# Sharing two TensorE clusters between a pair's outputs and the next pair's scores in a retention and feed-forward kernel

## The chip, the core and the metric

The kernel runs on one core of a Trainium2 chip. The metric is the device time of one execution in microseconds (us). Six runs of the kernel before the change gave a median of 300.57 us (299.53 to 300.97).

## What is computed

Eight batches with eight heads, 576 positions, head size 64: a causal retention layer without softmax, whose scores decay with a rate of their own for each head, and a feed-forward on its output with a squared ReLU between two matrix products.

```python
scores = scale * np.matmul(q, k.transpose(0, 1, 3, 2))
gamma = 1.0 - 2.0 ** (-5.0 - np.arange(H))
Dmat = np.where(rel >= 0, gamma[:, None, None] ** rel[None, :, :], 0.0)
attn = np.matmul(scores * Dmat, v)          # then laid out as x: 4608 x 512
h = x @ w_in                                # 512 x 2048
r = np.maximum(h, 0.0)
out = (r * r) @ w_out                       # 2048 x 512
```

## The kernel before

**Units and groups.** The 4608 positions are cut into 36 units of 128 positions (L123 to L128). Four full units cover positions 0 to 511 of a batch; the last 64 positions of two batches share one tail unit. The units are handled in 19 groups (L130): two of one unit, then seventeen pairs. Within a unit the retention works on two chunks of 64 positions. It is computed by chunks: inside a chunk scores, masked and multiplied by v; between chunks a running state of 64x64 for each head, which is multiplied by q. The decay is put into v (`vdec`, when v is cast) and into the output (`gam`), so that the mask is plain ones and zeros.

**The steps of a unit.** SP loads k, q and v as fp32 (`add_load`, L255). POOL casts them to fp16 (`add_unit`, L312). For units from 8 on a transposing DMA, issued by SP too, makes `kqT`, the transposed k and q (L346); for the first eight TensorE transposes them. Loads, transposes and stores stand in one queue on SP, which issues them in order; a transpose waits there for the cast of q, a store for its output.

**The two clusters of a group** (`add_ret`, from L369). All retention matmuls are small, 64x64x64, on a quarter of the TensorE array (`quad`, L305: `row` is the half of the partitions that is read, `col` the half that is written).

- The first cluster, `fa` (L379), computes the scores (`psc`, 16 small matmuls a unit) and the sums for the state (`psS`, 16 for each full unit). VectorE (DVE) then masks the scores into `rT` (L409) and forms the states `Rm` and `R` from the sums (L426 to L436).
- The second cluster, `fb` (L461), computes the outputs (`psO`): first a part from the states (up to 16 small matmuls a pair), in which row half a writes PSUM bank 1 - a; then a drain of TensorE; then the masked scores times v, in which row half c writes bank c, with the rest of the state part. DVE multiplies the outputs by `gam` into `xT` (L509).

PSUM has eight banks. Four belong to the feed-forward (`ps_ff`). The other four are two tiles of two banks of one kind, `pr` (`ps_ret`, L152), shared by scores, sums and the outputs of each unit.

**The feed-forward** (`add_ff`, L557). The first product (`ph`, L571) has 64 matmuls of 128x256 for a pair, ScalarE (ACT) applies ReLU (L579), ACT or DVE squares (L589, L591). From group 3 to group 17 the second product is done by Strassen's scheme (`add_strassen`, L630): seven products of eight matmuls of 128x256 (`po`, L664), DVE sums of their inputs (`gS`, L642), ACT and DVE putting the results together (L677, L687, L707). The other groups use the plain product (L612).

**Who sets the order.** The order on each engine is fixed when the program is built. Every piece of work is a task with an engine, a key, a planned duration, the tasks it depends on and the buffers it takes and gives back (`Schedule`, L16). `emit` plays the tasks through with the planned times: an engine that is free takes the ready task with the lowest key. The instructions are then written in the order in which the tasks started in that plan. On the chip each engine runs its own list in order, whatever the true times are. The plan counts 1.2 us for a load on SP, 2.0 for a transpose and 4.0 more until it has landed. A key counts slots: 2 x 16 slots (`L`) for a unit of the feed-forward. In `add_ret` the first cluster of a group has key `base + 3`, the second `base + 24`, with `base` two units and 20 slots (`EARLY`) ahead of the group's own feed-forward, so that the feed-forward of earlier groups stands between and around the clusters.

Of the kernel before, what the change touches and what calls it, by code (L numbers as in the profile page):

```python
# [101 lines left out]
def kernel(  # L102
# [46 lines left out]
    u_pool = ctx.enter_context(tc.tile_pool(name="u", bufs=1))  # L149
    r_pool = ctx.enter_context(tc.tile_pool(name="r", bufs=3))  # L150
    ps_ff = ctx.enter_context(tc.tile_pool(name="ps_ff", bufs=4, space=bass.MemoryType.PSUM))
    ps_ret = ctx.enter_context(tc.tile_pool(name="ps_ret", bufs=2, space=bass.MemoryType.PSUM))  # L152

    ctx.enter_context(tc.manual_schedule())

# [53 lines left out]
    WARM = 48  # L209
    EARLY = 20  # L210
    SQ_ACT = (0, 1, 2, 3, 4, 5, 6)
    XBAR = 8
    FIRST = ["u0", "u1", "u2", "u3", "w0", "w1", "w2", "w3", "w4", "w5", "w6", "w7"]
    sched = Schedule(dict(ff=4, pr=2, g=3, ld=5, wst=4, kq=7, v16=7, rT=4, x=3, rl=3, o=4, p1=1, u2=1, u4=1,
                          R=6, Rm=6, kqT=6))
    add = sched.add
    tile_of = {}
# [91 lines left out]
    def half(x):  # L309
        return slice(64 * x, 64 * x + 64)  # L310
# [55 lines left out]
            T["kqT", u].append(e)  # L366


    def add_ret(g):  # L369
        us = sorted(groups[g])  # L370
        n = len(us)
        base = (us[0] - n) * L - EARLY
        for u in us:
            add_unit(u, base - L + 4 * (u - us[0]))
        full = [u for u in us if units[u][0] == "full"]
        sc = lambda s: slice(256 * s, 256 * (s + 1))


        def fa():  # L379
            tile_of["psc", g] = ps_ret.tile([P, 2, 512], FP32, name="psc", tag="pr")  # L380
            for s, u in enumerate(us):
                kT = tile_of["kqT", u]
                ps = tile_of["psc", g][:, :, sc(s)].rearrange("p a (n i) -> p a n i", i=64)
                for hp in range(NP):
                    for a, c in ((0, 0), (1, 1), (0, 1), (1, 0)):
                        quad(ps[half(c), a, hp, :], kT[half(a), hp, half(c)], kT[half(a), NP + hp, half(c)], a, c)
            if full:
                tile_of["psS", g] = ps_ret.tile([P, 2, 512], FP32, name="psS", tag="pr")
            for s, u in enumerate(us):
                if u not in full:  # L390
                    continue
                ps = tile_of["psS", g][:, :, sc(s)].rearrange("p c (n i) -> p c n i", i=64)
                for hp in range(NP):
                    for c, a in ((0, 0), (1, 1), (0, 1), (1, 0)):
                        h = 4 * (hp // 2) + 2 * a + hp % 2
                        quad(ps[half(a), c, hp, :], tile_of["kq", u][half(c), 0, half(2 * hp + a)],
                             tile_of["v16", u][half(c), h, :], c, a)
        casts = sum((T["casts", u] for u in us), [])
        A = add("PE", base + 3, 0.2 + 0.145 * (n + len(full)), fa, deps=sum((T["kqT", u] for u in us), casts),
                acq=("pr", "pr") if full else ("pr",))  # L400
        for u in us:
            sched.free("kq", [A])


        ms = []
        for s, u in enumerate(us):
            def fm(s=s, u=u):
                t = tile_of["rT", u] = work.tile([P, 2, NP, 64], FP16, name="rT", tag="rT")
                nc.vector.tensor_tensor(  # L409
                    out=t, in0=tile_of["psc", g][:, :, sc(s)].rearrange("p a (n i) -> p a n i", i=64),  # L410
                    in1=mask.rearrange("p (o r i) -> p o r i", o=1, r=1).to_broadcast([P, 2, NP, 64]), op=ALU.mult)
            ms.append(add("DVE", base + 5 + s, 0.7, fm, deps=[A] + ms[-1:], acq=("rT",)))
        sched.free("pr", ms[-1:])


        chain = []
        for s, u in enumerate(us):
            if u not in full:
                continue
            c0 = units[u][2] == 0  # L420

            def fr0(s=s, u=u, c0=c0):
                t = tile_of["Rm", u] = st_pool.tile([P, NP * D], FP16, name="Rm", tag="Rm")
                x = tile_of["psS", g][:, 0, sc(s)]
                if c0:
                    nc.vector.tensor_copy(out=t, in_=x)  # L426
                else:
                    nc.vector.tensor_tensor(out=t, in0=x, in1=tile_of["R", u - 1], op=ALU.add)

            def fr1(s=s, u=u):  # L430
                t = tile_of["tmp", u] = work.tile([P, NP * D], FP32, name="stmp", tag="stmp", bufs=1)
                nc.vector.tensor_tensor(out=t, in0=tile_of["psS", g][:, 1, sc(s)], in1=tile_of["Rm", u], op=ALU.add)

            def fr2(s=s, u=u):
                t = tile_of["R", u] = st_pool.tile([P, NP * D], FP16, name="R", tag="R")
                nc.vector.tensor_tensor(  # L436
                    out=t.rearrange("p (n d) -> p n d", d=D), in0=tile_of["tmp", u].rearrange("p (n d) -> p n d", d=D),
                    in1=dec128.rearrange("p (n o) -> p n o", o=1).to_broadcast([P, NP, D]), op=ALU.mult)
            r0 = add("DVE", base + 5.1 + s, 0.42, fr0, deps=[A] + chain[-1:] + ([] if c0 else [T["R", u - 1]]),
                     acq=("Rm",))  # L440
            if not c0:
                T["Rread", u - 1].append(r0)
            r1 = add("DVE", base + 5.2 + s, 0.42, fr1, deps=[r0])
            r2 = add("DVE", base + 5.3 + s, 0.35, fr2, deps=[r1], acq=("R",))
            chain += [r0, r1, r2]
            T["Rm", u], T["R", u], T["Rread", u] = r0, r2, []
        if full:
            sched.free("pr", [chain[-2]])

        def states(u):
            kind, b, c = units[u]
            if kind == "tail":
                return {0: ("R", u - 5), 1: ("R", u - 1)}
            r = {1: ("Rm", u)}
            if c:
                r[0] = ("R", u - 1)
            return r

        def fb():  # L461
            begun = set()

            def put(u, c, h, lhsT, rhs, row):
                col = h % 2
                ps = tile_of["psO", u][half(col), c, half(h // 2)]
                quad(ps, lhsT, rhs, row, col, start=(u, c, col) not in begun)
                begun.add((u, c, col))

            def inter(u, other):  # L470
                st = states(u)
                for n in range(2):
                    for a, b in ((0, 0), (1, 1), (0, 1), (1, 0)):
                        c = a ^ other
                        if c in st:
                            x = 2 * n + b
                            put(u, c, 4 * n + 2 * a + b, tile_of[st[c]][half(a), half(x)],
                                tile_of["kqT", u][half(a), NP + x, half(c)], a)
            for u in us:
                tile_of["psO", u] = ps_ret.tile([P, 2, 512], FP32, name="psO", tag="pr")  # L480
                inter(u, 1)

            nc.tensor.drain()
            for u in us:
                for m in range(NP):
                    for c, b in ((0, 0), (1, 1), (0, 1), (1, 0)):
                        h = 2 * m + b
                        put(u, c, h, tile_of["v16", u][half(c), h, :], tile_of["rT", u][half(c), m % 2, 2 * (m // 2) + b, :], c)
                inter(u, 0)
        reads = [T[x] for u in us for x in states(u).values()]  # L490
        Bt = add("PE", base + 24, 0.2 + 0.29 * n, fb, deps=ms + reads, acq=("pr",) * n)
        for u in us:
            sched.free("kqT", [Bt])
            sched.free("v16", [Bt])
            sched.free("rT", [Bt])
            for name, ru in states(u).values():
                if name == "R":
                    T["Rread", ru].append(Bt)
                else:
                    sched.free("Rm", [Bt, chain[-2]])  # L500

        xs = []
        for u in us:
            s = groups[g].index(u)

            def fx(u=u, s=s):
                if ("x", g) not in tile_of:
                    tile_of["x", g] = x_pool.tile([P, NP, n * P], FP16, name="xT", tag="xT")
                nc.vector.tensor_tensor(  # L509
                    out=tile_of["x", g][:, :, s * P:(s + 1) * P].rearrange("p n (c i) -> p c n i", c=2),  # L510
                    in0=tile_of["psO", u][:, :, 0:256].rearrange("p c (n i) -> p c n i", i=64),
                    in1=gam[units[u][0]], op=ALU.mult)
            xs.append(add("DVE", base + 27 + u - us[0], 0.7, fx, deps=[Bt] + xs[-1:], acq=() if xs else ("x",)))
            sched.free("pr", xs[-1:])
            T["x", u] = xs[-1]

# [200 lines left out]
            sched.free("o", [st])  # L719

    for g in range(len(groups)):
        add_ret(g)
    for u in range(NU):
        if ("Rread", u) in T:
# [34 lines left out]
```

## Time and profile before

| what | value |
|---|---|
| median of six runs | 300.57 us (299.53 to 300.97) |
| the profiled execution, its own time | 300.97 us |
| its span, first to last instruction | 299.3 us |
| DVE, scores masked (L409), 36 times | 684 ns each |
| DVE, outputs scaled (L509), 36 times | 683 ns each |
| TensorE, small matmuls of scores, sums and outputs (L306) | 576, 512 and 1088 |
| ACT idle, waiting for `ph` | 51.0 us |
| POOL idle, waiting for v, q and k to land | 44.1, 36.4 and 31.3 us |
| transposes to `kqT`, issue to landing, median of 28 | 4.3 us |

The span is what the profile covers; 1.67 us of the execution lie around it. In the lists of groups a row has the line of the kernel, the engine, the operation and how often it ran, then busy time and the mean of one. A timeline merges neighbours of one kind: its second column runs from the first start to the last end. A TensorE matmul overlaps the next ones, so the pace is read from start to start and not from the duration of one.

### The profile page before, as it was taken

Reading aid. Unit: us, or ns where it says so; the run is one execution under the profiler, and the core shown is the slowest. Engines: PE = TensorE matmul, PEld = TensorE weight load, DVE = VectorE, ACT = ScalarE, POOL = GpSimd, SP = SyncE. Lnnn points to the kernel's source line nnn. Section 1 sums busy time; section 2 is a strip of 40 time slices with the busy share of each in tenths; the row PEclk is TensorE's granted clock in tenths of the full one; section 3 lists DMA queues with packets and bytes.
Section 4 is the critical chain, followed back from the end, with each engine's and each line's share of the span. In section 5 each row is a group of like instructions: output and inputs, shape, how many; then the busy total and the mean of one; then the engine's idle time right before and its main releaser. Section 6 shows DMA issues by size and latency. Waiting matters only on the chain.

```text
span 299.3 us, 10320 instructions
## 1 busy us (share of the span) xinstructions
PE 286.9 (96%) x4456; PEld 235.8 (79%) x4456; DVE 194.1 (65%) x409; ACT 187.0 (62%) x351; POOL 96.5 (32%) x125
## 2 busy tenths in 40 slices
PE   5986999999999999999999999999999999999995
PEld 2455964688888888888888888888888888888874
DVE  1377479785778848593959594959395959383410
ACT  4233973396667476766676666665757676657861
POOL 3433358453334151524242342334353410000000
PEclk9999999999999999999999999999999999999999
DMA  9999999889999999999999997999999960102012
GB/s 166 218 346 384 357 243 225 183 183 186 200 213 137 230 179 201 156 224 182 202 159 211 216 152 183 187 228 190 246 193 206 200 161 2 72 1 74 0 70 72
DMA packets 151742, 54.16 MB, mean 181 GB/s; under 512 B 142864, under 2 KB 143120, under 8 KB 151696
## 3 DMA queue, kind: packets, MB, share of 16 engines
q1 hardware_dynamic: 151248, 52.97, 89.8%
q8 instruction: 35, 0.57, 0.9%
q10 hardware_dynamic: 448, 0.52, 0.7%
q14 instruction: 11, 0.09, 0.1%
HBM read 36.70 MB, written 9.44 MB: 154 GB/s over the span
## 4 chain that ended last, share of the span: by engine, by line
PE 88%; DVE 7%; issue 2%; ACT 2%; POOL 0%; POOLq 0%; DVEq 0%
PE ph L571 40%; PE po L664 30%; PE psO L306 5%; PE po L612 4%; PE warm L226 4%; PE psc L306 2%; DVE wT L528 2%; PE psS L306 1%; DVE gS L642 1%; DVE gT L591 1%; ACT rl L579 1%; ACT gT L589 1%; PE psT L354 1%; DVE R L436 1%; DVE rT L409 0%
## 5 line engine op out<-in xcount | busy, mean ns | idle before, releaser
L571 PE MATMUL ph<-xT,w_in 128*128 128x256 f16 (+1 forms) x1216 | 139.5, 267 | 0.1
L571 PEld LDWEIGHTS <-w_in 128*128 128x128 f16 x1216 | 112.0, 98 | 13.6 <-POOL w_in L287 0.3
L579 ACT ACTIVATE rl<-ph 128x512 f16<-128x512 f32 x144 | 84.5, 589 | 55.6 <-PE ph L571 51.0
L589 ACT ACTIVATE gT<-rl 128x512 f16<-128x512 f16 x112 | 70.6, 630 | 3.5
L642 DVE TENSOR_TENSOR gS<-gT 128x512 f16<-128x512 f16 x60 | 31.2, 521 | 49.5 <-ACT gT L589 47.4
L332 POOL TENSOR_TENSOR v<-v,vdec_full 128x512 f16<-128x512 f32 x32 | 34.7, 1086 | 51.5 <-DMA v<-in_v_dram 40.1
L664 PEld LDWEIGHTS <-gS 128*128 128x128 f16 x480 | 46.3, 98 | 6.2 <-DVE gS L642 0.5
L664 PE MATMUL po<-wT,gS 128*128 128x256 f16 x360 | 49.1, 273 | 0.2 <-DVE gS L642 0.2
L664 PEld LDWEIGHTS <-gT 128*128 128x128 f16 x360 | 34.7, 98 | 4.2
L320 POOL CAST kq<-k 128x512 f16<-128x512 f32 x36 | 24.3, 675 | 35.8 <-DMA k<-in_k_dram 31.3
L320 POOL CAST kq<-q 128x512 f16<-128x512 f32 x32 | 22.7, 710 | 36.6 <-DMA q<-in_q_dram 36.4
L664 PE MATMUL po<-w_out,gT 128*128 128x256 f16 x240 | 31.3, 273 | 0.0
L409 DVE TENSOR_TENSOR rT<-psc,mask 128x512 f16<-128x512 f32 x36 | 24.5, 684 | 4.2 <-PE psc L306 4.2
L509 DVE TENSOR_TENSOR xT<-psO,gam_full 128x512 f16<-128x512 f32 x36 | 23.3, 683 | 3.9 <-PE psO L306 3.7
L591 DVE TENSOR_TENSOR gT<-rl 128x512 f16<-128x512 f16 x32 | 16.9, 532 | 12.9 <-ACT rl L579 12.7
L612 PE MATMUL po<-w_out,gT 128*128 128x512 f16 (+1 forms) x112 | 22.9, 349 | 0.3 <-ACT w_out L287 0.3
L677 ACT COPY u<-po 128x256 f32<-128x256 f32 x30 | 11.0, 366 | 14.6 <-PE po L664 14.5
L436 DVE TENSOR_TENSOR R<-stmp,dec 128x256 f16<-128x256 f32 x32 | 18.7, 584 | 1.0
L226 PE MATMUL warm<-junk,ident 128*128 128x512 f16 x48 | 15.0, 450 | 3.0 <-DVE junk L205 3.0
L642 DVE TENSOR_TENSOR gS<-gS,gT 128x512 f16<-128x512 f16 x30 | 16.9, 563 | 1.0
L612 PEld LDWEIGHTS <-gT 128*128 128x128 f16 x112 | 10.6, 98 | 7.7 <-issue 0.6
L687 DVE TENSOR_TENSOR o<-po,u 128x256 f32<-128x256 f32 x30 | 12.6, 419 | 6.1 <-PE po L664 4.4
(57 smaller groups left out, 243.9 us busy)
## 6 DMA issues: line engine op xcount, KB each, us to landing
k<-in_k_dram SPq DMA_DIRECT2D x32, 256.0 KB, 5.0
q<-in_q_dram SPq DMA_DIRECT2D x32, 256.0 KB, 4.6
v<-in_v_dram SPq DMA_DIRECT2D x32, 256.0 KB, 4.9
out_dram<-o SPq DMA_DIRECT2D x31, 256.0 KB, 3.0
wi<-in_moe_w_in_dram SPq DMA_DIRECT2D x4, 1024.0 KB, 11.5
wo<-in_moe_w_out_dram SPq DMA_DIRECT2D x4, 1024.0 KB, 9.0
k<-in_k_dram SPq DMA_DIRECT2D x8, 128.0 KB, 3.9
q<-in_q_dram SPq DMA_DIRECT2D x8, 128.0 KB, 4.2
```

Source lines behind the costliest of these rows:

```text
L226: nc.tensor.matmul(warm_ps[0], lhsT=ident, rhs=junk, start=True, stop=True)
L306: nc.tensor.matmul(out_, lhsT=lhsT, rhs=rhs, start=start, stop=True, skip_group_check=True, tile_position=(64 * row, 64 * col))
L320: op(out=out_.rearrange("p (n b a d) -> p n b a d", n=2, b=2, a=2), in_=in_.rearrange("p (n a b) d -> p n b a d", n=2, a=2))
L332: nc.gpsimd.tensor_tensor(out=t, in0=tile_of["v32", u], in1=vdec[kind].rearrange("p (h o) -> p h o", o=1).to_broadcast([P, H, D]), op=ALU. ...
L409: nc.vector.tensor_tensor(out=t, in0=tile_of["psc", g][:, :, sc(s)].rearrange("p a (n i) -> p a n i", i=64), in1=mask.rearrange("p (o r i) ...
L509: nc.vector.tensor_tensor(out=tile_of["x", g][:, :, s * P:(s + 1) * P].rearrange("p n (c i) -> p c n i", c=2), in0=tile_of["psO", u][:, :, ...
L571: nc.tensor.matmul(tile_of["ph", g, fb][:, j, :], lhsT=w_in16[:, m, fi * P:(fi + 1) * P], rhs=tile_of["x", g][:, m, :], start=(m == 0), st ...
L579: nc.scalar.activation(out=t, in_=tile_of["ph", g, fb], func=ACTF.Relu)
L589: nc.scalar.activation(out=t, in_=rl, func=ACTF.Square)
L612: nc.tensor.matmul(tile_of["po", u, lo], lhsT=tile_of["g", g][:, fi, s * P:(s + 1) * P], rhs=w_out16[:, fi, lo:hi], start=(fi == 0), stop= ...
L642: nc.vector.tensor_tensor(out=Sx(k, h), in0=in0(h), in1=in1(h), op=op)
L664: nc.tensor.matmul(tile_of["pb", g, bank], lhsT=left(i), rhs=right[:, i, :], start=(start and i == 0), stop=(i == HF - 1), skip_group_chec ...
```

## The change

The scores and sums of the next pair are computed together with the outputs of the present one. From group 9 (`JOIN`, the tenth) to group 17, a group has two clusters again, but filled differently:

- `f1`, key `base + 10`: the first part of the outputs of group g, then the scores of group g + 1.
- `f2`, key `base + 30`: the sums of group g + 1, then the second part of the outputs of group g.

Between the two parts of an output there is other work in place of the drain. Group 9 still has a cluster of scores and sums of its own before; group 18 has outputs with the drain, and groups 0 to 8 have the old two clusters. `f2` waits for the masks of both groups, since the sums are written to the PSUM tile from which the scores of g + 1 were read: the two tiles of kind `pr` become one of kind `prS` (scores, then sums) and one of kind `prO` (outputs of both units of a pair, side by side in the same two banks; before a group's first join also the sums). The casts of groups after 9 get a key two units earlier than the others, and are added to the plan ahead of everything else. The planned duration of an output cluster goes from 0.2 + 0.29 n to 0.45 + 0.2944 n for n units.

```diff
-    ps_ret = ctx.enter_context(tc.tile_pool(name="ps_ret", bufs=2, space=bass.MemoryType.PSUM))
+    ps_ret = ctx.enter_context(tc.tile_pool(name="ps_ret", bufs=1, space=bass.MemoryType.PSUM))
...
+    JOIN = 9
...
-    sched = Schedule(dict(ff=4, pr=2, g=3, ld=5, wst=4, kq=7, v16=7, rT=4, x=3, rl=3, o=4, p1=1, u2=1, u4=1,
+    sched = Schedule(dict(ff=4, prS=1, prO=1, g=3, ld=5, wst=4, kq=7, v16=7, rT=4, x=3, rl=3, o=4, p1=1, u2=1, u4=1,
...
+    QUAD = 0.0092
+    last_g = len(groups) - 1
+
+    def joined(g):
+
+        return JOIN <= g < last_g
...
+    def add_casts(g):
+        for u in units_of(g):
+            add_unit(u, base_of(g) - L * (2 if g > JOIN else 1) + 4 * (u - units_of(g)[0]))
+
+    def add_ret(g):
+        n = len(groups[g])
+        base = base_of(g)
+        if not joined(g - 1):
+            nf = len(full_of(g))
+
+            def fa():
+                emit_scores(g)
+                emit_sums(g, "prO")
+            t = add("PE", base + 3, 0.2 + 16 * QUAD * (n + nf), fa, deps=scores_deps(g) + sums_deps(g),
+                    acq=("prS", "prO") if nf else ("prS",))
+            for u in units_of(g):
+                sched.free("kq", [t])
+            after_scores(g, t, base + 5)
+            after_sums(g, t, base + 5, "prO")
+        if joined(g):
+            k = len(groups[g + 1])
+
+            def f1():
+                emit_out1(g)
+                emit_scores(g + 1)
+
+            def f2():
+
+                emit_sums(g + 1, "prS")
+                emit_out2(g)
+            t1 = add("PE", base + 10, 0.2 + QUAD * (8 * n + 16 * k), f1, deps=out1_deps(g) + scores_deps(g + 1),
+                     acq=("prO", "prS"))
+            after_scores(g + 1, t1, base + 11)
+            t2 = add("PE", base + 30, 0.2 + QUAD * (24 * n + 16 * len(full_of(g + 1))), f2,
+                     deps=[t1] + T["masked", g] + T["masked", g + 1] + sums_deps(g + 1), acq=("prS",))
+            for u in units_of(g + 1):
+                sched.free("kq", [t2])
+            after_outs(g, t1, t2, base + 30.4)
+            after_sums(g + 1, t2, base + 31, "prS")
+        else:
+            def fb():
+                emit_out1(g)
+                nc.tensor.drain()
+                emit_out2(g)
+            t = add("PE", base + 24, 0.45 + 32 * QUAD * n, fb, deps=T["masked", g] + out1_deps(g),
+                    acq=("prO",))
+            after_outs(g, t, t, base + 27)
```

`emit_scores`, `emit_sums`, `emit_out1` and `emit_out2` hold the small matmuls of the old `fa` and `fb` unchanged; `after_scores`, `after_sums` and `after_outs` hold the DVE work that followed them.

## The prediction

> **What bounds the kernel now.** I read the page first: busy time by engine and the chain that ended last.
>
> ```profile
> PE 286.9 (96%) x4456; PEld 235.8 (79%) x4456; DVE 194.1 (65%) x409; ACT 187.0 (62%) x351; POOL 96.5 (32%) x125
> ...
> PE 88%; DVE 7%; issue 2%; ACT 2%; POOL 0%; POOLq 0%; DVEq 0%
> ```
>
> TensorE sets the end. Next, its timeline around group 9, the first that the change joins (columns: start, time from first start to last end, instruction, count).
>
> ```profile
> 128.02 1.04 PE L664 MATMUL po<-wT,gS 128*128 128x256 f16 x8
> 128.99 0.45 PE L306 MATMUL psc<-kqT 64*64 64x64 f16 x32
> 129.26 0.30 PE L306 MATMUL psS<-v,kq 64*64 64x64 f16 x16
> 129.50 0.61 PE L571 MATMUL ph<-xT,w_in 128*128 128x256 f16 x4
> ...
> 133.87 0.60 PE L571 MATMUL ph<-xT,w_in 128*128 128x256 f16 x4
> 134.40 0.21 PE L306 MATMUL psO<-kqT,Rm 64*64 64x64 f16 x1
> ...
> 134.82 0.32 PE L306 MATMUL psO<-rT,v 64*64 64x64 f16 x16
> ...
> 135.32 1.05 PE L664 MATMUL po<-w_out,gS 128*128 128x256 f16 x8
> ...
> 142.76 1.04 PE L664 MATMUL po<-wT,gS 128*128 128x256 f16 x8
> 143.72 0.45 PE L306 MATMUL psc<-kqT 64*64 64x64 f16 x32
> 144.00 0.44 PE L306 MATMUL psS<-v,kq 64*64 64x64 f16 x32
> 144.37 1.05 PE L571 MATMUL ph<-xT,w_in 128*128 128x256 f16 x8
> ```
>
> Eight wide matmuls (128x256) take 0.875 us from start to start (144.37 to 145.25 is one such step), 0.1094 us each. From here on TensorE never waits: each stretch between clusters is that number times its matmuls. So time taken from a cluster is time taken from the end, and every wait put into TensorE's stream is added to it.
>
> What comes close behind is the supply. The loads and the transposes that make kqT are issued in order by SP:
>
> ```profile
> 128.36 1.24 SPq L346 DMA_TRANSPOSE kqT<-kq  x1
> 129.71 0.99 SPq L548 DMA_DIRECT2D out_dram<-o  x2
> 130.76 0.44 SPq L262 DMA_DIRECT2D k<-in_k_dram  x1
> 131.25 0.69 SPq L262 DMA_DIRECT2D q<-in_q_dram  x1
> 131.98 1.26 SPq L262 DMA_DIRECT2D v<-in_v_dram  x1
> 133.29 0.93 SPq L262 DMA_DIRECT2D k<-in_k_dram  x1
> 134.27 1.14 SPq L262 DMA_DIRECT2D q<-in_q_dram  x1
> 136.48 2.55 SPq L346 DMA_TRANSPOSE kqT<-kq  x1
> ```
>
> Counted from the first transpose (unit 8), these are the transpose of unit 18, two stores, the loads of unit 19, k and q of unit 20, and the transpose of unit 19 at 136.48. The answer for the tile kqT in a window around that last one gives its landing:
>
> ```profile
> DMA to landing us min/median/max: 5.0/5.0/5.0
> ```
>
> So kqT of unit 19 is there at 141.5, only 2.4 us before its scores (143.9, the second half of the 32 at 143.72). The same sum for unit 17 gives 128.4 against 129.1, for unit 15 114.1 against 114.3: no spare time. Supply gains slowly: from k of unit 18 (121.43) to k of unit 30 (200.3) SP issues 12 units in 78.9 us, 6.6 us each, while TensorE uses a unit in half of 14.87 us (143.72 to 158.59).
>
> **The change, part by part.**
>
> *The drain.* A cluster's price is the step between the wide matmuls around it less their own time. Scores and state sums, 64 small matmuls: 142.76 + 0.875 = 143.635 to 144.37, 0.735 us. The same with 48 (group 9): 128.895 to 129.50, 0.605; so 16 small ones more cost 0.13 us. Outputs, also 64, with the drain: 133.87 + 0.4375 = 134.31 to 135.32, 1.01 us. The drain is the difference, 0.28 us. After the change the clusters of a group hold 48 and 80 small matmuls: 0.605 + 0.865 = 1.47 us in place of 0.735 + 1.01 = 1.75. The number of clusters stays (20 from group 9 on, before and after), so entry and exit cost the same. Groups 9 to 17 are joined: 9 x 0.28 = **2.5 us less**. The small matmuls, their total and their operands' sizes are the same.
>
> *Scores moved forward.* In the changed order the first joined cluster stands 44 wide matmuls behind the scores of group 9, exactly where the outputs of group 9 stand now: its first matmul falls at 134.40 of the old clock. It holds 16 output matmuls, 16 scores of unit 18 and then those of unit 19, which read kqT of unit 19 first at 134.40 + 32 x 8.4 ns = 134.67. That was 143.9 before. TensorE runs in order, so all that is queued behind these scores waits too: the 20 wide matmuls up to the second cluster, the feed-forward after it, and through them ACT and DVE.
>
> When does kqT of unit 19 land? POOL's order of casts is unchanged. In SP's order only two stores and q of unit 20 move: now k19, store, q19, store, v19, k20, transpose, q20. q19 therefore goes at most one store (0.5 us) sooner than 131.25, lands 4.5 us later, is cast in 0.6; the transpose is issued between 136.0 and 136.5. Transposes between 100 and 140 us took 3.1 to 5.3 us to land; this one 5.0 with q20 ahead of it. I take 136.2 + 4.6 = 140.8 plus 0.1 for the wake-up; the ends are 139.1 and 141.9. The new wait is **6.2 us** (ends 4.4 and 7.2).
>
> *The later joins* need their kqT at 144.4, 159.0, 173.6, 188.2 and 202.6 (cumulated wide and small matmuls of the new order, no wait counted); with the old issue times they would land at 155.6, 166.3, 177.8, 193.1 and 208.3, that is 11.2, 7.3, 4.2, 4.9 and 5.7 late. The 11.2 shrinks: the transpose of unit 21 waited for q21, issued at 145.21 behind the transpose of unit 20 and two stores (143.15, 2.0 us); now q21 goes ahead of all three, and k22 and q22 behind. That is some 5 us sooner, about 6 late. The 7.3 loses a load and a store ahead of it, 1.5 us. All these lie under a delay that the first join has already brought, so I add nothing, with 1 us as the upper end.
>
> *The clock.* TensorE stood still for 6 us nowhere between the head and the end of the old run; its longest pause after the head, 1.5 us at 26.2, left the pace at once full. The other end is the head, where TensorE had done nothing for 3.05 us and 13 matmuls needed 5.5 us where four later need 0.65:
>
> ```profile
> 3.00:8.50 5.50, 5.45 (x13) 1.00 1.32 227
> 8.85:9.50 0.65, 0.65 (x4) 1.00 1.35 217
> ```
>
> That is 427 ns against 216 a piece (the granted clock reads 1.00 in both rows, so I go by the spacing): 13 x 0.211 = 2.7 us lost. After a 6 us wait the price lies between 0 and 2.7; the wait is nearer to the head's standstill than to 1.5 us, and I take **1.8**. [...]
>
> *The rest.* The second cluster needs both masks of the next pair: two of 0.68 us plus wake-up, 1.5 us, beside 2.19 us of wide matmuls at the first join and 4.8 or more at the later ones; without that cover it would cost up to 1 us a join. The next scores need the state sums read out: about 3.9 us of DVE work beside 6.1 us of feed-forward. In groups 4 to 6 the new outputs' cost in the planner moves the scores 0.9 to 2 us forward, into loads with 0.2 to 0.4 us to spare (unit 9: lands 75.0, used 75.4); the 0.5 us lost there is swallowed by the wait at the first join, which is set by a landing and not by when TensorE arrives.
>
> *Sum* on the profiled execution: span 299.3 - 2.5 + 6.2 + 1.8 = 304.8, and with the 1.67 around it (300.97 - 299.3) 306.5. The median before is 0.4 lower, so the forecast is **306.1 us**.
>
> **The rivals.** (1) *The wait without the clock*: the pace is full at once, -2.5 + 6.2: 304.3, from 302.5 to 305.0 with the landing's ends and the later joins. For it: pauses of 1.5 us cost nothing. Against: this is four times as long. (2) *The supply arrives in time*: one mechanism at one place, kqT of unit 19. If it lands by 134.7, nothing waits and the whole 2.5 us is kept: 298.1. It decides at 137.2: landing earlier makes the kernel faster. Against it: q19 itself landed at 135.8. For it: only that DMA times could shift with the new order from 95 us on. (3) *Halfway*: landing near 137, the wait eats the gain: 300.0 to 301.2. (4) *The queue feeds back*: outputs now come 6 to 8 us later; a store waiting for them on SP holds the loads behind it, and later joins wait again: 309.5 to 314. Against: the stores of units 12 to 16 now go out 5 to 12 us after their data, and the new order puts stores behind loads. (5) *The change doesn't do what it says*: the drain's 0.28 us comes back where outputs and scores now meet; then the forecast is 308.6. Against: scores and sums follow each other today with no gap (143.72 to 144.00 is 32 steps of 8.8 ns).
>
> **How the numbers follow.** Forecast, with (5) inside its upper part, 0.50, from 305 to 309.5; (1) 0.28; (2) 0.10; (3) 0.05; (4) 0.07. The range takes in the forecast and (1): 302.5 to 309.5; outside lies 0.22 less what of (3) and (4) falls within, just under 0.20. About 0.2% (0.6 us) is what a measurement can tell from no change: faster 0.11, same 0.04, slower 0.85.
>
> **What would show it.** Right: in the new timeline one TensorE wait of 4 to 7 us inside the score matmuls near 135, released by the transpose; matmuls after it spaced at twice 0.109 us for a few us; no gap of 0.28 us inside the later clusters, and a period of 14.6 in place of 14.87 us. Wrong: no wait there, or kqT of unit 19 landing before 137; a second long wait at 150 or 165; the pace at 0.109 at once after the wait; or clusters of 80 that take 1.1 us and not 0.87.

## The result, and the profile after

| | before | after |
|---|---|---|
| median of the runs (us) | 300.57 (39 runs, 299.53 to 303.04) | 303.48 (18 runs, 300.62 to 306.52) |
| profiled execution (us) | 300.97 | 304.94 |
| its span (us) | 299.3 | 303.2 |

The ratio is 1.0069, with a 95% interval from 1.0050 to 1.0088; executions more than 1.5% above the fastest of their kernel are left out of it, which is why it is smaller than the ratio of the medians. The kernel became slower, by 2.1 us by the ratio and 2.9 us by the medians. The forecast was 5.5 us slower: the sign is right, the size is 1.9 to 2.7 times what came.

The page of the changed kernel answers the two lines shown of before. A DMA, absent from the old chain that ended last, now has a share in it: about half of its 6% is the load of q of unit 19 and its transpose (4.6 and 4.8 us), the other half and the SyncE queue (SPq) are loads at the start.

```profile
PE 287.1 (95%) x4456; PEld 236.0 (78%) x4456; DVE 189.2 (62%) x409; ACT 186.7 (62%) x351; POOL 95.8 (32%) x125
...
PE 81%; DMA 6%; DVE 4%; SPq 4%; ACT 2%; issue 2%; POOL 1%
```

What TensorE waited for from 128 us to the end (engine, line, operation waited for: sum, number, longest, in us):

```profile
PE psc L307 <- DMA kqT<-kq: 4.2, 1, 4.2
PE po L733 <- DVE gS L711: 0.4, 1, 0.4
```

It is one wait, at the scores of unit 19. TensorE's timeline there (start, time from first start to last end, instruction, count, wait in brackets):

```profile
133.96 0.30 PE L307 MATMUL psc<-kqT 64*64 64x64 f16 x16
138.45 0.43 PE L307 MATMUL psc<-kqT 64*64 64x64 f16 x16 [4.19 <-DMA kqT<-kq]
138.81 1.89 PE L733 MATMUL po<-w_out,gS 128*128 128x256 f16 x8
140.50 1.91 PE L733 MATMUL po<-wT,gT 128*128 128x256 f16 x8
142.20 1.06 PE L640 MATMUL ph<-xT,w_in 128*128 128x256 f16 x4
...
144.31 0.94 PE L640 MATMUL ph<-xT,w_in 128*128 128x256 f16 x7
```

The scores of unit 18 run at 133.96, those of unit 19 start at 138.45: 4.38 us from the start of the last of the former to the start of the first of the latter. Times called a standstill below are such steps; a wait in brackets is 0.2 to 0.3 us less. Then eight wide matmuls take 1.69 us (138.81 to 140.50) where before eight took 0.875. The table by stretches gives the clock for it (busy time and instructions of TensorE, its weight loads, VectorE, ScalarE, GpSimd; granted clock as a share of the full one, DMA share, GB/s):

```profile
135.00:138.00 3.00, 0.00 (x0) 0.00 (x0) 0.00 (x0) 0.00 (x0) 1.54 (x2) 0.88 1.21 118
138.00:141.00 3.00, 2.55 (x27) 1.88 (x28) 1.29 (x2) 0.26 (x1) 0.69 (x3) 0.50 1.34 222
141.00:144.00 3.00, 3.00 (x71) 2.10 (x73) 0.43 (x1) 0.78 (x3) 2.20 (x3) 0.50 1.30 241
144.00:147.00 3.00, 3.00 (x61) 2.69 (x54) 2.46 (x6) 2.13 (x4) 0.00 (x0) 0.98 1.08 95
```

A row of 3 us at 0.88 holds an estimated 0.72 us of half clock, twice what it lacks. So the granted clock is halved during the standstill, at about 137.3, and stays so until about 144.1, for 6.8 us. Twenty wide matmuls at 213 instead of 109 ns (2.1 us), the second cluster of 80 at 1.36 instead of 0.87 us (0.5) and the sixteen scores (0.1) make 2.7 us lost.

Last, SyncE's queue ahead of the transpose of unit 19, which before was issued at 136.48:

```profile
124.77 2.27 SPq L347 DMA_TRANSPOSE kqT<-kq  x1
127.09 0.58 SPq L263 DMA_DIRECT2D k<-in_k_dram  x1
127.78 0.51 SPq L617 DMA_DIRECT2D out_dram<-o  x1
128.34 0.43 SPq L263 DMA_DIRECT2D q<-in_q_dram  x1
...
133.59 1.24 SPq L347 DMA_TRANSPOSE kqT<-kq  x1
```

It is issued 2.9 us sooner than in the old trace and lands 4.8 us after its issue, at 138.4. The account of the profiled span, all from start-to-start steps on TensorE: 299.3, less 2.5 for nine drains, less 0.6 by which this execution was ahead at the first joined cluster (it begins at 133.8, not 134.4), plus 4.4 for the wait, 2.7 for the clock and 0.1 more than before in waits for VectorE: 303.4, against 303.2 measured. The 0.6 can't be put down to the new order: in a second trace of the old kernel, below, the same cluster begins at 133.9, in one of the changed kernel at 134.1.

### The profile page after: what moved, and what is told of

It is laid out like the page before. It is cut to its first block, busy times and chain, and to the rows that moved or that the text cites. A ratio compares the mean times of both kernels' runs of the same rounds, so it can differ in the third digit from the quotient of the medians.

```text
span 303.2 us, 10320 instructions
## 1 busy us (share of the span) xinstructions
PE 287.1 (95%) x4456; PEld 236.0 (78%) x4456; DVE 189.2 (62%) x409; ACT 186.7 (62%) x351; POOL 95.8 (32%) x125
## 4 chain that ended last, share of the span: by engine, by line
PE 81%; DMA 6%; DVE 4%; SPq 4%; ACT 2%; issue 2%; POOL 1%
PE ph L640 39%; PE po L733 30%; PE psO L307 4%; SPq L263 4%; PE po L681 4%; DMA wi<-in_moe_w_in_dram 3%; DVE wT L597 2%; DMA kqT<-kq 2%; PE psc L307 2%; PE psS L307 2%; DMA q<-in_q_dram 2%; ACT rl L648 1%; ACT gT L658 1%; DVE gT L660 1%; DVE gS L711 1%
## 5 line engine op out<-in xcount | busy, mean ns | idle before, releaser
L711 DVE TENSOR_TENSOR gS<-gT 128x512 f16<-128x512 f16 x60 | 27.2, 453 | 39.8 <-ACT gT L658 39.2
L733 PEld LDWEIGHTS <-gT 128*128 128x128 f16 x360 | 35.4, 99 | 4.5
L321 POOL CAST kq<-q 128x512 f16<-128x512 f32 x32 | 21.6, 676 | 38.2 <-DMA q<-in_q_dram 38.2
L530 DVE TENSOR_TENSOR xT<-psO,gam_full 128x512 f16<-128x512 f32 x36 | 24.0, 686 | 10.3 <-PE psO L307 10.1
L660 DVE TENSOR_TENSOR gT<-rl 128x512 f16<-128x512 f16 x32 | 18.5, 587 | 12.2 <-ACT rl L648 12.0
L776 ACT COPY o<-po 128x256 f32<-128x256 f32 x15 | 5.5, 366 | 19.4 <-PE po L733 19.4
L681 PEld LDWEIGHTS <-gT 128*128 128x128 f16 x112 | 10.7, 98 | 8.0 <-issue 0.6
L733 PE MATMUL po<-w_out,gS 128*128 128x256 f16 x120 | 16.5, 283 | 0.0
```

Of the source, the lines that this page charges most:

```text
L321: op(out=out_.rearrange("p (n b a d) -> p n b a d", n=2, b=2, a=2), in_=in_.rearrange("p (n a b) d -> p n b a d", n=2, a=2))
L530: nc.vector.tensor_tensor(out=tile_of["x", g][:, :, s * P:(s + 1) * P].rearrange("p n (c i) -> p c n i", c=2), in0=tile_of["psO", g][:, :, ...
L660: nc.vector.tensor_tensor(out=t, in0=rl, in1=rl, op=ALU.mult)
L681: nc.tensor.matmul(tile_of["po", u, lo], lhsT=tile_of["g", g][:, fi, s * P:(s + 1) * P], rhs=w_out16[:, fi, lo:hi], start=(fi == 0), stop= ...
L711: nc.vector.tensor_tensor(out=Sx(k, h), in0=in0(h), in1=in1(h), op=op)
L733: nc.tensor.matmul(tile_of["pb", g, bank], lhsT=left(i), rhs=right[:, i, :], start=(start and i == 0), stop=(i == HF - 1), skip_group_chec ...
```

## The experiments

The theory that I tested: the drains are worth their 2.5 us; the loss is one transpose that lands after the scores that now want it, and the half clock that follows; how late it lands differs from execution to execution. Rivals: the clock falls because of the joined clusters and not of the standstill; the drain's time comes back elsewhere; the new order of VectorE's work takes the gain.

**The old kernel again** (for the landing).

> The kernel before once more, for its trace: does kqT of unit 19 land at the same time in another execution? It landed at 141.5 us in the first trace; in the four traces that use the new order of loads it landed at 138.4, 137.7, 140.2 and 136.9. If the new order of loads made it earlier, it lands at 141 to 142 here too. If it is the spread of the DMA from run to run, it lands anywhere from 137 to 142. Time 300 to 301.

300.76 us, span 299.0. SyncE's queue, with its transpose of unit 19:

```profile
128.96 0.95 SPq L262 DMA_DIRECT2D q<-in_q_dram  x1
...
134.71 2.72 SPq L346 DMA_TRANSPOSE kqT<-kq  x1
```

Same program, same place in the queue, but q of unit 19 is issued at 128.96 and not 131.25, the transpose at 134.71 and not 136.48. It landed at 140.4 instead of 141.5, so the same program differs by 1.8 us in the issue and 1.1 in the landing. Of these two traces, the one that I forecast from is that with the later supply.

**The changed kernel again.**

> The changed kernel once more, for a second trace. [...]

303.26 us, span 301.6. TensorE's one wait from 128 us on:

```profile
PE psc L307 <- DMA kqT<-kq: 3.6, 1, 3.6
```

and by stretches, in the columns of above:

```profile
135.00:138.00 3.00, 0.00 (x0) 0.00 (x0) 0.11 (x1) 0.00 (x0) 1.29 (x2) 1.00 1.17 120
138.00:141.00 3.00, 2.88 (x28) 2.10 (x29) 1.29 (x2) 0.37 (x1) 1.00 (x2) 0.52 1.35 217
141.00:144.00 3.00, 3.00 (x99) 2.47 (x97) 1.19 (x3) 1.23 (x2) 1.89 (x3) 0.91 1.27 240
```

The step is 3.75 us, the landing 138.1; the half clock ends at 141.5 and costs 14 wide matmuls their double pace, 1.6 us with the scores. The second cluster is at 0.87 us again. The span is 1.7 us shorter than in the first trace: 0.6 less wait, 1.1 less loss by the clock; a later start of the cluster (0.3) and shorter waits for VectorE nearly cancel. The wait was 3.6 us and not 4.2 again, and by the rows at 0.52 and 0.91 the half clock lasted 3.4 us, where the first trace has 6.8.

**Scores from data that is there.** The scores of a joined group read the key transpose of two units before, so the values of those units are others; nothing else is left out.

```diff
-            kT = tile_of["kqT", u]
+            kT = tile_of["kqT", u - 2 if joined(g - 1) else u]
```

> The scores that a joined cluster computes read kqT of the pair before (which TensorE already uses in the same cluster) in place of their own, so the result is not the reference's; orders, loads and counts stay. My theory: the change loses by one wait, for kqT of unit 19 at the first joined cluster (4.4 us in the profile after), and by the half clock behind it (2.8 us), and gains 9 drains of 0.28 us. Then no wait is left there, the clock stays full from 20 us to the end, and the span is 299.3 - 2.5 - 0.6 (which the stretch before group 9 already gained) = 296.2, a time of 297.8. The rival, that joined clusters cost as much as they save or that the moved loads and stores lose the time, expects 300 or more with no wait there.

300.3 us (10 runs), ratio 0.9996 (0.9973 to 1.0019), against 297.8 expected (a span of 296.2): missed. The profiled execution has 299.32, span 297.6, the fastest of the ten, and no wait for a transpose from 128 us on; the joined clusters take 0.602 and 0.869 us:

```profile
PE po L733 <- DVE gS L711: 0.7, 3, 0.3
```

So the wait and its clock were the loss (about 3 us of the median). But without them only 1.6 us of span are gained in the trace, not 3.1, and over ten runs nothing that can be told: most of what the drains should give doesn't show in the times. What TensorE waits for in that trace from 128 us on is the line above. The steps from start to start are longer than its 0.7 us: 0.52, 0.36, 0.44 and 0.56 us ahead of Strassen products that wait for VectorE's sums (1.4 us in all over a wide matmul's 0.109; before had one of 0.4, against the forecast's "TensorE never waits"), and at the head a wait for w_in of 2.6 us; the mean granted clock of this execution is 0.994. The trace answers one more question: without the first wait, the scores of unit 23 would have come 2.5 us and those of unit 29 2.3 us before their transposes landed (161.4 against 158.9, 205.4 against 203.1); that of unit 21 had not been issued (144.45) when its scores ran (144.3). The first wait pays for the later ones, as the forecast said.

**TensorE kept busy while it waits**, with 16 and with 36 filling matmuls between the outputs and the scores of the first joined cluster (the diff is that of the first).

```diff
+        if g == JOIN + 1:
+            for i in range(16):
+                nc.tensor.matmul(tile_of["psc", g][:, i % 2, :], lhsT=ident, rhs=junk, start=True, stop=True)
```

> Sixteen full matmuls of 128x512 on zeros stand between the outputs and the scores of the first joined cluster, written to the place of the scores before these; they fill 3.5 us of the wait. My theory, that the half clock comes from the standstill: the scores of unit 19 still start when kqT lands, the standstill shrinks from 4.4 to about 1 us, no matmul behind it runs at twice the spacing, and the time falls by the 2.8 us of the half clock against the changed kernel's profiled run: about 302 (range 300.5 to 303, as the landing varies). The rival, that the clock falls for another reason or that filling does not count, expects the half clock again and 304 to 306.

305.33 us (4 runs), ratio 1.0153 (1.0121 to 1.0186). The filling took 3.5 us, but the landing was at 140.2 in this trace, so 2.4 us of standstill were left, and half pace followed all the same: eight wide matmuls took 0.89 us, the next eight 1.52, so that it began an estimated 1.3 us after the end of the standstill:

```profile
140.25 0.32 PE L307 MATMUL psc<-kqT 64*64 64x64 f16 x16 [2.20 <-DMA kqT<-kq]
140.50 1.05 PE L736 MATMUL po<-w_out,gS 128*128 128x256 f16 x8
141.39 1.73 PE L736 MATMUL po<-wT,gT 128*128 128x256 f16 x8
142.91 1.06 PE L643 MATMUL ph<-xT,w_in 128*128 128x256 f16 x4
```

The expectation is missed, in the time (about 302) and in the clock: I had believed that 2.4 us were too short.

> The changed kernel with 36 matmuls of a 512-column block ahead of the scores of unit 19, at the first joined cluster; what they write is overwritten, so nothing else is changed. In the run with 16 of them they took 3.5 us and 2.4 us of standstill were left behind them; 36 take 36 x 0.218 = 7.8 us and reach past every landing of the key transpose seen so far (136.9 to 140.8). Theory: the half-clock windows come from the standstill, not from the change of kind of work: no standstill over 0.5 us at this place, no half-clock window after it, the next joined cluster (80 matmuls) at 0.87 us, and the span at that of before, 299.0 to 299.3, plus 7.8 of filling less 2.5 of drains less 0.6 gained earlier, plus 0.2 to 1.5 of waits for VectorE: 304.0 to 305.4. [...]

306.13 us (one execution), span 304.4 as expected, and TensorE waits for no transpose. By stretches:

```profile
133.00:136.00 3.00, 3.00 (x35) 1.80 (x34) 1.65 (x5) 0.76 (x2) 1.18 (x1) 1.00 1.18 121
136.00:139.00 3.00, 3.00 (x16) 1.37 (x14) 0.00 (x0) 0.00 (x0) 1.19 (x2) 1.00 1.11 232
139.00:142.00 3.00, 3.00 (x16) 1.27 (x13) 0.00 (x0) 0.00 (x0) 1.69 (x3) 1.00 1.31 195
142.00:145.00 3.00, 3.00 (x68) 2.33 (x70) 1.71 (x3) 0.39 (x2) 1.33 (x2) 1.00 0.97 190
```

The clock stays at 1.00 and the cluster of 80 takes 0.870 us. The filling adds 7.99 us to its cluster. From the first scores of group 9 to the last matmul this trace takes 172.26 us (128.67 to 300.93), 164.3 without the filling; the two traces of the old kernel take 166.8 and 167.1. Less their waits for VectorE (0.3 us against 0.4 and 0.6) the difference is 2.4: the nine drains. In the trace with the scores from earlier data the stretch is 165.3, with 1.0 us more of waits for VectorE. So here the half clock goes with the standstill and not with the joined clusters, and in these two traces the drains are worth their price when nothing waits. Why the ten runs with earlier data gain less than their trace stays open.

**The drains put back** between the outputs and the scores that now share a cluster.

```diff
                 emit_out1(g)
+                nc.tensor.drain()
                 emit_scores(g + 1)
```

> The changed kernel with the drain put back between the outputs and the scores of each joined cluster. My theory: each of the nine clusters of 48 takes 0.88 us in place of 0.60, as the old output clusters did; where TensorE waits anyway (the first join) it is hidden. So the profile shows eight or nine gaps of 0.28 us, and the time is 2.2 to 2.5 us above the changed kernel in a run with the same wait and clock, 303 to 307. The rival, that the drain cost only the end of the matmuls ahead of it and so nothing net: clusters of 0.60 us.

307.64 us (4 runs), ratio 1.0215 (1.0173 to 1.0256), a little above the expected range. Clusters of 44 and 48 take 0.87 to 0.89 us instead of 0.60 at the eight later joins, and at all nine a step of 274 to 297 ns stands between outputs and scores: the drain, as sized. In this trace the transpose landed at 136.9 and the wait was 2.1 us; TensorE's timeline:

```profile
136.93 0.32 PE L307 MATMUL psc<-kqT 64*64 64x64 f16 x16 [2.05 <-DMA kqT<-kq]
137.18 1.89 PE L734 MATMUL po<-w_out,gS 128*128 128x256 f16 x8
138.86 1.88 PE L734 MATMUL po<-wT,gT 128*128 128x256 f16 x8
```

Behind this standstill, 2.24 us from start to start, eight wide matmuls took 1.68 us, and the granted clock was 0.86 from 135 to 138 us and 0.57 from 138 to 141: an estimated 3.4 us of half clock. By the ratio the nine drains would be worth 4.4 us, by the traces' steps 2.5; with four runs, and waits that differ by 2 us, I take the steps.

**The joined clusters later in the plan**: the planner's keys of the two clusters, and of the DVE work behind them, 30 higher.

```diff
-            t1 = add("PE", base + 10, ...
+            t1 = add("PE", base + 40, ...
-            t2 = add("PE", base + 30, ...
+            t2 = add("PE", base + 60, ...
```

> Both keys of a joined group are 30 slots later (40 and 60, and those of its DVE work with them), so the scores of unit 19 fall some 3.9 us later in TensorE's order, at 138.3 of the old clock, and the later ones 9 us later. My theory: a wait of 0 to 2 us at the first join, too short for the clock to fall, none later, and the drains saved: 297.5 to 299.5, faster than both kernels. The rival, that the joined clusters themselves cost: 300.5 or more without any wait. If the wait moves along with the join (supply bound by the order on SP and not by time), 302 or more.

310.8 us (6 runs), ratio 1.0342 (1.0302 to 1.0382). The waits of TensorE from 128 us on:

```profile
PE po L733 <- ACT u L746: 3.7, 8, 0.5
PE po L733 <- DVE gS L711: 3.7, 7, 0.8
PE psc L307 <- DMA kqT<-kq: 1.8, 1, 1.8
```

Expectation missed. The step at the transpose was 2.0 us, and the mean granted clock of the profiled execution is 0.994; some 1.3 us a group, in steps, were lost to waits for VectorE's Strassen sums and for evictions of products (`u`, `o`) by ScalarE and VectorE. That the joined clusters' DVE work in its new place holds these up is likely, but wasn't tested.

**A plan that knows the landing**: the planner reckons 4 us for it. One kernel says 12 from unit 18 on, another 10, 12, 16 and 12 by units.

```diff
-  after=4.0
+  after=4.0 if u < 18 else 12.0
```

> The changed kernel, with one figure of the planner's changed: from unit 18 on a transpose counts as landed 12 us after its issue slot and not 4. Nothing that is computed or loaded changes; TensorE's order does: the first joined cluster stands 7.4 us later in it, at 141.8 of the old clock, the next at 149.9 and 162.2, and from 202 on nothing moves. My theory, that the loss is the plan's too early supply and nothing else: no wait at the first join and no half clock there; a wait of 0 to 4 us may be left at the scores of unit 27 (189.6 in the order, landed 192 to 194 in the traces so far). Time 298 to 301.5. The rival, that clusters in this place cost on their own, or that the wait moves along with the cluster: 302 or more, with a wait of over 2 us at the first join.

302.15 us (12 runs), ratio 1.0030 (0.9999 to 1.0062): 0.65 above the expected range. No wait at the first join, as expected, but no gain came. The waits of TensorE from 128 us on, three kinds of about a microsecond each:

```profile
PE psc L307 <- DMA kqT<-kq: 0.9, 1, 0.9
PE psS L307 <- DVE rT L469: 0.8, 1, 0.8
PE po L733 <- DVE gS L711: 0.7, 2, 0.5
```

> The changed kernel with one edit in the plan: the planner reckons 10 us for the landing of the key transpose for units 18 to 21, 12 for 22 to 25, 16 for 26 to 29 and 12 after, instead of 4, so that the first joined clusters are planned at 140.1, 148.6, 162.2, 176.8 and 192.7 us, where the transposes have landed, and the clusters stand 2.6 to 4.9 us apart. Theory: the wait and its half clock were most of the loss, and a plan that knows the landing gets rid of them without new waits of more than 1 us in all; then 9 drains of 0.28 us less that: 298.5 to 300.0 us, ratio 0.993 to 0.998. Rival: the order on VectorE (masks of the joined scores ahead of the gate sums) costs as much as the drains gave, wherever the clusters stand; then 300.2 to 301.5 us, ratio 0.999 to 1.003, as in the runs that join from group 15 or reckon 12 us for all.

303.74 us (6 runs), ratio 1.0080 (1.0049 to 1.0112): expectation missed, and slower than the rival said too: no wait for a transpose and yet no gain. The first joined cluster stood at 140.2, after the landing (137.0), but the second then came 2.6 us later, and VectorE had both masks, a run of sums, the feed-forward's inputs and the read-out of the state sums to do in a row. TensorE's timeline behind the second cluster:

```profile
143.53 1.27 PE L733 MATMUL po<-wT,gS 128*128 128x256 f16 x10
146.87 2.48 PE L640 MATMUL ph<-xT,w_in 128*128 128x256 f16 x16 [2.06 <-DVE xT L530]
```

A standstill of 2.3 us, and 1.2 us after its end sixteen wide matmuls at half pace (148.1 to 151.5); the granted clock was 0.84 from 146 to 149 us and 0.59 from 149 to 152. In this trace, moving the first cluster back to where the data is took away the distance that VectorE needed before the second.

**Joins from a later group on** (JOIN = 15, and 12 twice).

> The same change from group 15 on (three joined groups), where kqT landed 11 us ahead of its use in the profile after. My theory: no wait of over 1 us, the clock stays full, three drains (0.85 us) saved, some 0.3 us of it lost again to later sums of DVE: 299.5 to 300.5, the same as before or just faster. The rival, that a joined cluster costs in itself: above 300.6 without a wait.

301.12 us (12 runs), ratio 0.9991 (0.9964 to 1.0017): no difference that can be told, no wait for a transpose. The time is above the expected 299.5 to 300.5, as was the old kernel's beside it (301.17). Three drains are worth 0.85 us; waits for VectorE of 0.23, 0.41, 0.35 and 0.89 us stand against them.

> The same change from group 12 on (six joined groups). The first joined cluster needs kqT of unit 25 at 179.0 (landed 177.8 before), the second that of unit 27 at 187.9 (landed 193.1 before). My theory: no wait at the first, 2 to 5 us at the second, with a half clock behind it where the wait is over 2 us, against 1.7 us of drains: 300 to 304. The rival, that only the first joined group waits, whichever it is: a wait at group 12 and none at 13.

304.67 us (4 runs), ratio 1.0107 (1.0060 to 1.0154): above the expected range. The profiled one (305.61) had a mean granted clock of 0.943, so its time says nothing; the other three took 303.84 to 305.30 at 0.989 to 0.994. Its trace waits 0.3 us for the transpose of unit 27.

> The changed kernel joining from group 12 on instead of 9 (six joins instead of nine), once more, since the earlier profile of it had a granted clock of 0.949 from end to end. Theory: at group 12 the transposes are in time; six drains of 0.28 us go (1.7 us), 0.5 us come back as a wait for the transpose of unit 27 and 0.6 to 1.2 us as waits for VectorE's gate sums; 299.8 to 301.0 us, ratio 0.997 to 1.001. Rival: the joins are worth their drains wherever no half clock follows; then 298.9 to 299.4 us, ratio 0.994 to 0.996.

303.58 us (11 runs, 301.32 to 308.14), ratio 1.0076 (1.0036 to 1.0115): slower, against both theories. Even the two runs at a clock of 1.00 took 301.32 and 301.38. In the profiled execution, one of the two slowest (306.87), the place of the wait has moved, to the scores of unit 27; first TensorE's waits, then SyncE's queue:

```profile
PE psc L307 <- DMA kqT<-kq: 5.8, 1, 5.8
PE po L733 <- DVE gS L711: 0.2, 1, 0.2
```

```profile
180.89 2.53 SPq L347 DMA_TRANSPOSE kqT<-kq  x1
183.52 1.17 SPq L621 DMA_DIRECT2D out_dram<-o  x2
184.74 0.59 SPq L263 DMA_DIRECT2D q<-in_q_dram  x1
...
190.22 1.25 SPq L347 DMA_TRANSPOSE kqT<-kq  x1
```

q of unit 27 stands behind a transpose of 2.5 us and two stores, its transpose goes out at 190.22 and lands at 194.4; the scores were due at 188.7. In the run before with the same program the same scores were due at 192.2 and the transpose landed at 192.5. So the 5.5 us between the two waits are 3.6 of TensorE being sooner and 1.9 of the landing being later.

> The same kernel, joining from group 12, with the read-out of the state sums planned at base + 60 instead of base + 31: on VectorE the two gammas' products that feed the feed-forward then stand together ahead of the sums, and in some groups the gate sums stand ahead of part of the sums' read-out. Theory: the waits of TensorE for VectorE's gate sums come from the 4.7 us of products and read-out that a joined pair of row tiles puts ahead of them; with part of it behind, these waits fall from 0.6 to 1.2 us to under 0.4 us in all, and the time is 0.3 to 0.8 us below that of its twin. Rival: these waits come from ScalarE's gates and stay within 0.3 us of the twin's; the time is the same.

```diff
-            after_sums(g + 1, t2, base + 31, "prS")
+            after_sums(g + 1, t2, base + 60, "prS")
```

305.49 us over 12 runs from 298.79 to 310.14; the ratio (1.0001, 0.9958 to 1.0044) rests on four of them and says little. Its trace stands still for 5.5 us at the same transpose, and for 0.33 and 0.51 us at VectorE's sums against 0.34 in its twin: expectation missed, and the cause of those waits stays open. The best single time, 298.79, had a clock of 1.00; what it did not wait for was not recorded.

No version beat the old kernel by more than can be told from no change.

## Why the prediction was right in its direction and wrong in its size

*The drain*: right. Clusters of 48 and 80 take 0.602 and 0.870 us (0.605 and 0.865 forecast), three steps of 14.6 us lead from the scores at 209.4 to those at 253.2, and putting the drains back brings steps of 0.27 to 0.30 us. In the times of many runs, though, these 2.5 us were never seen by themselves.

*Scores moved forward*: this is the step that failed, in its size. The wait is where and what the forecast said, the scores of unit 19 behind the transpose, but 6.2 us were forecast and 4.4 and 3.75 measured; in the trace with the drains put back it was 2.2. The term was the difference of two times, a landing and a need, and the landing was taken from one trace with a late supply. "The transpose is issued between 136.0 and 136.5": in the thirteen traces with the new order of loads ahead of this place it went out between 132.65 and 136.3, in nine of them before 134.3; in the second trace of the old kernel at 134.7. It landed between 136.9 and 140.8, in nine of the thirteen under the lower end of 139.1 (140.4 and 141.5 in the old kernel), in the first trace of the changed kernel 4.8 us after its issue. Against the 134.1 to 134.5 at which the scores then stood (134.67 in the forecast), the landings of the six traces with these joins and the old plan stand for waits of 2.2 to 6.0 us. The 6.0 is from the run with 16 filling matmuls, where the transpose was issued at 136.3 and landed at 140.2: there the forecast's supply came about. "At most one store sooner" compared with the late trace; against the second old trace q of unit 19 is indeed 0.6 us sooner in the profiled new one. How much of the 2 to 3 us the order gave and how much is the execution's chance, two traces of the old kernel can't tell. With the terms of the second trace of the changed kernel in place of the forecast's, 300.57 - 2.5 + 3.75 + 1.6 is 303.4, against a median of 303.48.

*The later joins*: right that they add nothing, for the reason given; the slack at units 21 and 23 was 3.0 and 3.8 us in the profile after, and without the first wait and its clock, 7.1 us together, it would have been negative.

*The clock*: right that it falls, 1.8 us forecast, 1.6 and 2.7 measured. The 1.8 was a guess between 0 and 2.7, so that it lies near is in part luck: the half clock lasted 3.4 us in the second trace of the changed kernel and 6.8 in the first, and the traces don't say which execution gets how much (behind the standstill of 4.4 us it was 6.8; in the last run, which stood for 5.5, the clock of 0.91 from 190 to 210 us makes an estimated 3.6). The runs without a profile fit this: all eighteen have a mean granted clock under 1.00, nine 0.994, which makes an estimated 3.6 us of half clock in 300 us (300.62 to 303.37 us), the others 0.989 or 0.983 (303.59 to 306.52). Some of it may be at the head. In the trace with the 3.75 us the half clock ended 3.4 us behind the wait; after 4.4 us it took 5.7.

*The rest*: the cover for masks and sums was costed at nothing. In the changed kernel as it is that is right (0.1 us more in one trace, less in the other). Where the first join doesn't wait, steps that wait for VectorE add 0.3 us (36 filling matmuls), 1.4 (earlier data), 1.9 (joins from group 15) and 3.8 (the plan by units). The forecast's "up to 1 us a join" without cover holds for the masks (0.9 us in the plan with 12 us) but not for VectorE's outputs `xT`, which cost 2.2 us in one step of the plan by units.

*The rivals*: the median of 303.48 lies nearest to the number of the wait without the clock (304.3), but that mechanism is refuted, by the rows at 0.50 and by the matmuls at 213 ns: a shorter wait and a half clock add up to much the same. "The supply arrives in time" was to decide at 137.2. Two of the six landings were earlier, at 136.9, and one of them (the drains put back) still had its half clock behind a wait of 2.2 us: the deciding point had left out that so short a wait could bring a clock loss (1.7 us there). The queue did not feed back: no later transpose was waited for. In the profiled run's own terms, 304.8 of span became 303.2: 1.8 less wait, 0.6 from an earlier start, 0.9 more clock.

## What to carry to other kernels

Before work is moved forward in an engine's list, compare the times at which its operands land with the time at which it will stand (here all that was queued behind the scores stood too: TensorE ran no matmul from 135 to 138 us), and take the landings from several executions: here the same transpose landed anywhere within 4 us, so that one trace gave a wait of 6.2 us where 2.2, 3.75 and 4.4 were measured. Where the supply is the limit behind the limit, a gain ahead of it can be paid back at the next operand: joins from group 12 on moved the wait to unit 27, and a later place in the plan traded it for waits for VectorE and ScalarE. In mid-kernel here, standstills of TensorE of 2.24, 3.75 and 4.4 us cost another 1.7, 1.6 and 2.7 us by the clock.

## What the runs showed of the hardware

- TensorE's standstills, from start to start, and the granted clock behind them: 1.5 us at 26.2 in the old kernel and 1.9 us at 20.5 in the changed one, 1.00 in the rows behind both; 2.24 us with the drains put back, 0.57 from 138 to 141; 2.3 us in the plan by units, 0.59 from 149 to 152; 3.75 and 4.4 us in the two traces of the changed kernel, 0.52 and 0.50 from 138 to 141. With 16 filling matmuls 2.4 us were followed by eight wide matmuls in 1.52 us, with 36 and no standstill the rows read 1.00.
- The half clock, estimated from the rows, lasted 3.4 us behind 2.24, 2.3 and 3.75 us, and 6.8 us behind 4.4 us and behind the wait of 5.8 us in the second run that joins from group 12 (0.98 from 190 to 192, 0.50 from 192 to 198, 0.81 from 198 to 200). It began 1.2 us before the end of the standstill of 4.4 us, 2.5 before that of the wait of 5.8, and 1.2 and 1.3 after those of 2.3 and 2.4. Its length doesn't follow from the standstill alone: in the last run the row from 190 to 210, with TensorE busy for 14.67 of 20 us, reads 0.91, which makes 3.6 us.
- One execution had a mean granted clock of 0.943 (the first of those that join from group 12).
- Issue to landing of the same key transpose was 5.0 and 5.7 us in the two traces of the old kernel and 4.8 in the first of the changed one, in kernels whose transfers around it are the same but for their order.
